# Two late edits in a fused RWKV attention and cosine feed-forward kernel: the last two half copies change buffers and order, and six checks with their vote move to an earlier place

## The chip, the cores and the metric

The kernel runs on one core of one Trainium2 chip. A core has five engines that each work through a queue in order: TensorE (PE, with its weight loads shown as PEld), VectorE (DVE), ScalarE (ACT), GpSimd (POOL) and SyncE (SP), whose queue here only issues DMA transfers. The metric is device microseconds (us) of one execution.

## The reference, cut to what matters

Batch 4, 8 heads, 768 steps, head size 48. A linear attention with decay `w` gives 3072 rows of 384 values; these go through a feed-forward layer of width 2048 whose gate is `h * cos(h)`:

```
state_t = w_t * state_(t-1) + k_t v_t ;  y_t = r_t (state_(t-1) + u k_t v_t)
h = x @ w_in ;  out = (h * cos(h)) @ w_out
```

The fast way of computing the decay is valid only for some inputs. So the kernel also looks at all of `w` (is any absolute value over 1?) and at the chunks' products of decays (is any too small?). A vote over both decides at the very end, in one branch that every engine takes, whether a slow loop over single steps redoes the whole output. With the inputs here it does not.

## The kernel before, in words

The 3072 rows are 24 chunks of 128 steps, two chunks to a block. A block's feed-forward is 8 units of 256 hidden columns, so there are 96 units. After a start written out token by token, the loop at L788 runs through **slots** t = 16 to 97. Slot t holds the first products of unit t (`mm1`, L577) and the second products of unit t - 2 (`mm2`, L595). Between them stands the gate of the unit, six steps on three engines: I (ScalarE, L540, reads the product bank), S (VectorE, L543), N (ScalarE, a sine, L556), M (VectorE, L557, the last reader of the product bank), H (ScalarE, L170, writes `gs`) and L (GpSimd, two halves, L173). There are two product banks, so `mm1` of slot t + 2 needs M of slot t to be over.

The attention of later chunks is spread over the same slots by the rows of PLAN. On VectorE it is a backward scan `e` (L282), a reciprocal and a forward scan `f` (L287, L288), the products `k` and `r` (L299, L301), `u` (L320), the sum `c` (L324), the decayed state `d` (L357) and twelve masked copies `P` (L395), which put the scores into the `asb` buffers. On PE it is the scores (L381), and for each block once the *own products* (L462, L468, from `asb`) and the *past products* (L490, L496), both ahead of `mm1` in the seventh of every eight slots; for the last block that is slot 86. When a block's last unit is over, ScalarE copies the two accumulators out (`ob`, L609) and SP sends them.

In each queue of PE, VectorE, ScalarE and GpSimd the instructions stand in the order of the program (L781). Only SP's order and the choice of a free buffer are the planner's.

The search for a large `w` is `check_decays` (L526 to L532): six pieces of 768 KB, each loaded by SP into a buffer of the five-fold ring `tt`, which also holds the chunks' inputs. VectorE takes the maximum of the piece (L531) and merges it into `wmax` (L532). A piece is checked after the events of its slot: with CHECK = 12, in slots 84 to 89. `take_vote` has two parts. The first (slot 91) is three small VectorE instructions that make `vote` and `low` (L769, L771, L773). The second (slot 92) is two one-column products on PE into a bank `pv` (L762, L763), and two VectorE instructions that make `bad` (L765, L766), which the branch at the end reads.

In the trace, `mm1` of slot 79 starts at 419.70 us, of slot 80 at 423.89, of 81 at 428.08, of 82 at 432.26, of 83 at 436.45, of 84 at 442.23, of 85 at 446.53 and of 86 at 453.73.

The last block's second accumulator is copied out in halves of 192 columns: VectorE copies the left one into `ob` and ScalarE the right one into `other` (L606, L607), both buffers of the ring `rr`; SP and ScalarE each send one half.

Of the kernel before, what the change touches and what calls it, by code (L numbers as in the profile page):

```python
# [10 lines left out]
F32 = mybir.dt.float32  # L11
# [7 lines left out]
AF = mybir.ActivationFunctionType  # L19
ALU = mybir.AluOpType  # L20
ET = mybir.EngineType

C = 128
# [17 lines left out]
W_SCALE = 2.0 ** 8  # L41
# [46 lines left out]
LAST = "mm1 I S N M", "mm1 I S N M mm2 h l", "mm2 h l"  # L88
CHECK = 12
PAIR = "0011010101010101"  # L90
NEEDS = dict(decay="load", lr="load", lv="load", diag="lr", d="decay", a="decay diag", t="decay",
             o="a lv", s="t d lv", p="o d")
# [3 lines left out]
def rwkv_cos_ffn(ctx: ExitStack, tc: tile.TileContext, tr, tn, tv, u, ut, wts, w, rkw, vst, us, xs, out):  # L96
    nc = tc.nc
    NG = tr.shape[0]
    TRW = tr.shape[2]
    DM = out.shape[1]  # L100
# [12 lines left out]
    def bank(kind, shape, name):  # L113

        tags = BANKS[stage[0]]
        turn[kind] += 1
        return ps.tile(shape, F32, tag=tags[kind][turn[kind] % len(tags[kind])], name=name)
# [3 lines left out]
    def buf(tag, shape, dtype, name=None, pool=sb):  # L121
        return pool.tile(shape, dtype, tag=tag, name=name or tag, bufs=BUFS.get(tag, 1))
# [37 lines left out]
    def engines(codes):  # L160
        E.update({k: {"v": nc.vector, "p": nc.gpsimd, "a": nc.scalar, "s": nc.sync}[e] for k, e in codes.items()})
# [61 lines left out]
    atts, outs, xts, units, accs = {}, {}, {}, {}, {}  # L223
# [302 lines left out]
    def check_decays(n):  # L526

        ww = buf("tt", [128, w.shape[1] // WCH], F32, "ww")
        nc.sync.dma_start(out=ww, in_=w[:, n * w.shape[1] // WCH:(n + 1) * w.shape[1] // WCH])
        top = buf("top", [128, 1], F32)  # L530
        nc.vector.tensor_reduce(out=top, in_=ww, axis=mybir.AxisListType.X, op=ALU.max, apply_absolute_value=True)  # L531
        nc.vector.tensor_tensor(out=wmax, in0=wmax, in1=top, op=ALU.max)  # L532
# [49 lines left out]
    def mm2(t):  # L582
        i, u = seq[t]
        if u == 0:
            if i < 2:
                stage[0] = 1 if i else 2
            tags = ("a2", "h2") if i == 1 else ("acc0", "acc1")
            accs[i] = [ps.tile([C, 512], F32, tag=x, name="acc") for x in tags]
        gs = units.pop(t)
        todo = [(a, b, fi, j) for a, b in PASSES for fi in range(FU) for j in range(BLK)]  # L590
        at_end = i == NBLK - 1 and u == NU - 1
        if at_end:
            todo.sort(key=lambda x: x[3])
        for a, b, fi, j in todo:
            nc.tensor.matmul(out=accs[i][j][:, :DM], lhsT=gs[:, a, fi, j * C:(j + 1) * C],  # L595
                             rhs=wgt[u * FU + fi][:, 1, b],
                             start=u == 0 and fi == 0 and a == 0 and b == 0, stop=u == NU - 1 and fi == FU - 1 and a == 1)
        if u == NU - 1:
            if i == 1:
                stage[0] = 3  # L600
            for j in range(BLK):
                ob = buf("rr", [C, DM], F32, "ob")
                with tc.high_priority(offset=HP):
                    if at_end and j:
                        other = buf("rr", [C, DM], F32, "other")
                        nc.vector.tensor_scalar(out=ob[:, :DM // 2], in0=accs[i][j][:, :DM // 2], scalar1=1.0 / W_SCALE ** 2, scalar2=None, op0=ALU.mult)  # L606
                        nc.scalar.activation(other[:, DM // 2:], accs[i][j][:, DM // 2:DM], AF.Copy, scale=1.0 / W_SCALE ** 2)  # L607
                    else:
                        nc.scalar.activation(ob, accs[i][j][:, :DM], AF.Copy, scale=1.0 / W_SCALE ** 2)  # L609
                chunk = order[i * BLK + j]  # L610
                if at_end and j:
                    nc.sync.dma_start(out=out[chunk * C:(chunk + 1) * C, :DM // 2], in_=ob[:, :DM // 2])
                    nc.scalar.dma_start(out=out[chunk * C:(chunk + 1) * C, DM // 2:], in_=other[:, DM // 2:])
                else:
                    E["qo"].dma_start(out=out[chunk * C:(chunk + 1) * C, :], in_=ob)

# [8 lines left out]
    slots = len(seq)  # L625
# [34 lines left out]
    def up(n):  # L660

        if n == 0 and up1[0] < slots:
            if up1[0] - up1[1] > LAG + 1:
                up(1)
            mm1(up1[0])
            up1[0] += 1
        elif n == 1 and up1[1] < up1[0]:
            mm2(up1[1])
            up1[1] += 1

    def events(i, row, t):
        for e in row.split():
            n, _, d = e.partition("+")
            if e == "mm1":
                up(0)
            elif e == "mm2":
                if up1[1] <= t - LAG:
                    up(1)
            elif e in "ISNMHLhl":
                at = (e.upper(), t - e.islower())  # L680
                if at in parts:
                    parts.pop(at)()
            elif n in "efrkmucPKXnd":
                at = i * (1 if n in "Xn" else BLK) + int(d)
                for m in dict(e=("decay",), m=("diag",), d=("d",)).get(n, ()):
                    att(at, m)
                for key in dict(f=(("f", at), ("W", at)), c=(("c", at), ("A", at)), d=(("d", at), ("pp", at)),
                                X=[(x, (at, side)) for x in ("xh", "xl") for side in range(2)]).get(n, ((n, at),)):
                    if key in parts:
                        parts.pop(key)()  # L690
            else:
                att(i * (1 if n in "osp" else BLK) + int(d), n)
# [66 lines left out]
    def take_vote(last):  # L759
        if last:  # L760
            pv = bank("a", [C, 512], "pv")
            nc.tensor.matmul(out=pv[:1, 0:1], lhsT=told["vote"], rhs=ones[:, 0:1], start=True, stop=True)  # L762
            nc.tensor.matmul(out=pv[:1, 1:2], lhsT=ones[:R, 0:1], rhs=told["low"], start=True, stop=True)  # L763
            votes = cst.tile([1, 1], F32, name="votes")
            nc.vector.tensor_reduce(out=votes, in_=pv[:1, 0:2], axis=mybir.AxisListType.X, op=ALU.add)  # L765
            nc.vector.tensor_copy(out=bad, in_=votes)  # L766
            return
        told["vote"] = vote = cst.tile([128, 1], F32, name="vote")
        nc.vector.tensor_single_scalar(out=vote, in_=wmax, scalar=1.0, op=ALU.is_gt)  # L769
        least = cst.tile([R, 1], F32, name="least")  # L770
        nc.vector.tensor_reduce(out=least, in_=wholes.rearrange("p g a -> p (g a)"), axis=mybir.AxisListType.X, op=ALU.min)  # L771
        told["low"] = low = cst.tile([R, 1], F32, name="low")
        nc.vector.tensor_single_scalar(out=low, in_=least, scalar=LEAST, op=ALU.is_le)  # L773
# [7 lines left out]
    with tc.manual_schedule(engines={ET.PE, ET.DVE, ET.Activation, ET.Pool}):  # L781
        with tc.manual_schedule(engines={ET.SP}):
            nc.scalar.copy(out=mask, in_=maskf)
            for token in START.split():
                at_first(token)
        engines(LATER)
        up2 = up1[0]
        for t in range(up2, slots + LAG):  # L788
            n = t - up2
            if t == slots - 2:  # L790
                E["g0"] = nc.vector
            row = FIRST[n] if n < len(FIRST) else PLAN[t % NU]
            events(t // NU, row if t < slots - 2 else LAST[t - slots + 2] if t <= slots else "mm2", t)
            if t >= slots - CHECK and n_checked[0] < WCH:
                check_decays(n_checked[0])
                n_checked[0] += 1
            if t == slots - CHECK - 1:
                nc.vector.tensor_reduce(out=halves, in_=ident[:R96, :R96].rearrange("p (h d) -> p h d", d=HD),
                                        axis=mybir.AxisListType.X, op=ALU.add)
            if t in (slots - 5, slots - 4):  # L800
                take_vote(t == slots - 4)
        while up1[1] < slots:
            up(1)
    assert not parts, list(parts)
# [172 lines left out]
```

## Time and profile before

| what | us |
|---|---|
| median of three runs | 507.45 (505.34 to 508.76) |
| the profiled execution | 505.55 |
| its span | 503.8 |
| PE busy | 496.7 (99%) |
| DVE busy | 389.5 (77%) |
| ACT busy | 256.5 (51%) |
| POOL busy | 204.7 (41%) |

The span is the time from the first to the last recorded instruction of the profiled execution; 1.75 us lie outside it. Busy shares are means over the whole span. Times of day in the text are us from the start of the span.

### The profile page before, as it was taken

The page shows a single profiled execution, that of the slowest core. Times are in us where ns is not written, and L with a number is a line of the kernel's source. Part 1 is how long each engine was busy: PE and PEld are TensorE (multiplying, and loading weights), DVE is VectorE, ACT ScalarE, POOL GpSimd, SP SyncE. Part 2 cuts the span into 40 slices and gives each one's busy share as a digit, 9 for nine tenths or more (in the row PEclk, how much of TensorE's full clock was granted, in tenths as well). Part 3 has the DMA queues.
Part 4 walks back from the last instruction along what each step waited for, and adds up shares of the span by engine and source line. Part 5 has one row for each costly group of instructions (what it writes and reads, how often), then busy time and mean ns, then how long its engine had stood idle before and what let it go on. Part 6 is the DMA issues. An engine that isn't in the chain of part 4 may idle for free.

```text
span 503.8 us, 13400 instructions
## 1 busy us (share of the span) xinstructions
PE 496.7 (99%) x5654; PEld 482.6 (96%) x5654; DVE 389.5 (77%) x685; ACT 256.5 (51%) x444; POOL 204.7 (41%) x274
## 2 busy tenths in 40 slices
PE   8999999999999999999999999999999999999997
PEld 8889999999999999999999999999999999999997
DVE  7998999687979868868868957967957966587633
ACT  2889788525344444445445335435534545544543
POOL 4434646435445344335333424524623633423330
PEclk9999999999999999999999999999999999999999
DMA  8989540242141051051051132214205203013001
GB/s 284 411 315 337 224 161 2 64 163 96 54 174 64 1 196 62 3 196 62 1 176 53 33 125 72 64 50 147 65 8 188 64 2 126 33 63 129 31 2 35
DMA packets 17327, 54.64 MB, mean 108 GB/s; under 512 B 2032, under 2 KB 8688, under 8 KB 17264
## 3 DMA queue, kind: packets, MB, share of 16 engines
q1 hardware_dynamic: 17120, 53.64, 30.1%
q8 instruction: 46, 0.75, 0.6%
q14 instruction: 17, 0.14, 0.1%
q10 hardware_dynamic: 144, 0.10, 0.1%
HBM read 49.02 MB, written 4.72 MB: 107 GB/s over the span
## 4 chain that ended last, share of the span: by engine, by line
PE 75%; DVE 12%; issue 4%; DMA 3%; ACT 3%; POOL 1%; SPq 1%; ACTq 0%; DVEq 0%; POOLq 0%
PE acc L595 33%; PE ph L577 32%; PE pa L381 2%; DVE rr L543 2%; DVE rr L557 2%; DMA tt<-tr 2%; PE py L462 2%; DMA raw<-wts 1%; PE py L468 1%; DVE tt L288 1%; PE py L496 1%; DVE ee L282 1%; PE pst L427 1%; DVE asb L395 1%; PE pt L404 1%
## 5 line engine op out<-in xcount | busy, mean ns | idle before, releaser
L173 POOL TENSOR_TENSOR gs<-rr,gs 128x256 fp32r<-128x256 f32 x188 | 154.2, 840 | 231.4 <-ACT gs L170 209.8
L577 PE MATMUL ph<-xT,w 128*128 128x256 f32 x1728 | 219.8, 281 | 0.2 <-DVE w L204 0.2
L595 PE MATMUL acc<-w,gs 128*128 128x384 f32 x1152 | 216.2, 337 | 0.2 <-DVE rr L557 0.2
L577 PEld LDWEIGHTS ph<-xT,w 128*128 128x128 f32 x1728 | 212.6, 188 | 3.4 <-issue 1.2
L595 PEld LDWEIGHTS acc<-w,gs 128*128 128x128 f32 x1152 | 196.2, 188 | 1.1 <-issue 0.6
L556 ACT ACTIVATE rr<-rr,quarter 128x512 f32<-128x512 f32 x96 | 69.4, 723 | 87.1 <-DVE rr L543 86.9
L543 DVE SCALAR_TENSOR_TENSOR rr<-rr,ph 128x512 f32<-128x512 int32 x96 | 65.5, 682 | 51.6 <-ACT rr L540 49.9
L170 ACT CAST gs<-rr 128x512 fp32r<-128x512 f32 x88 | 54.6, 620 | 66.3 <-DVE rr L557 40.2
L540 ACT ACTIVATE rr<-ph 128x512 int32<-128x512 f32 x96 | 57.3, 596 | 51.8 <-PE ph L577 51.4
L557 DVE TENSOR_TENSOR rr<-rr,ph 128x512 f32<-128x512 f32 x96 | 65.5, 682 | 22.0 <-ACT rr L556 19.7
L334 POOL TENSOR_SCALAR_AFFINE_SELECT asb<-cd 128x512 f32<-128x512 f32 x48 | 35.5, 766 | 52.4 <-DVE cd L324 35.1
L395 DVE COPY_PREDICATED asb<-turned_mask,pa 64x128 f32<-64x128 uint8 (+1 forms) x108 | 33.6, 347 | 1.8 <-POOL asb L334 0.3
L282 DVE TENSOR_TENSOR_SCAN ee<-tt,one_e 112x516 f32<-112x516 f32 (+1 forms) x25 | 32.7, 1313 | 2.2 <-POOL asb L334 1.2
L288 DVE TENSOR_TENSOR_SCAN tt<-tt,inj 112x516 f32<-112x516 f32 x24 | 30.3, 1262 | 0.8
L173 DVE TENSOR_TENSOR xT<-py,xT 128x384 fp32r<-128x384 f32 x22 | 11.4, 552 | 21.2 <-ACT xT L170 21.2
L194 ACT ACTIVATE top<-raw 128x768 f16<-128x768 bf16 x16 | 17.4, 1090 | 3.7 <-DMA raw<-wts 2.6
L170 ACT CAST xT<-py 128x384 fp32r<-128x384 f32 x24 | 10.4, 483 | 17.1 <-PE py L496 17.0
L462 PE MATMUL py<-asb,v 128*32 128x128 f32 x384 | 18.0, 276 | 0.3 <-DVE asb L392 0.2
L468 PE MATMUL py<-asb,v 128*32 128x128 f32 x384 | 17.3, 273 | 0.0
L202 DVE CUSTOM_DVE_ANT_0 h<-h,top 128x1536 uint16<-128x1536 uint16 x16 | 16.1, 1005 | 0.9 <-ACT top L194 0.9
L170 ACT COPY past<-dd 48x192 f32<-48x192 f32 x40 | 14.0, 349 | 2.7 <-DVE dd L357 2.4
L381 PEld LDWEIGHTS pa<-tt 48*64 48x64 f32 x576 | 12.9, 133 | 2.2 <-issue 2.2
(90 smaller groups left out, 370.7 us busy)
## 6 DMA issues: line engine op xcount, KB each, us to landing
tt<-tr SPq DMA_DIRECT2D x22, 770.5 KB, 7.0
raw<-wts SPq DMA_DIRECT2D x16, 767.8 KB, 7.1
rk<-tn SPq DMA_DIRECT2D x18, 384.0 KB, 3.5
v<-tv SPq DMA_DIRECT2D x24, 224.0 KB, 3.6
ww<-w SPq DMA_DIRECT2D x6, 768.0 KB, 5.2
out<-ob SPq DMA_DIRECT2D x23, 192.0 KB, 2.0
tt<-tr SPq DMA_DIRECT2D x4, 256.0 KB, 3.5
tt<-tr SPq DMA_DIRECT2D x1, 258.5 KB, 3.2
```

The costliest lines, as they stand in the source:

```text
L170: (nc.scalar.copy if E[name] is nc.scalar else E[name].tensor_copy)(out=out, in_=in_)
L173: E[name].tensor_tensor(out=out, in0=full, in1=high.bitcast(F32), op=ALU.subtract)
L282: nc.vector.tensor_tensor_scan(out=ee[:, pairs].rearrange("p a t -> p (a t)")[:, ::-1], data0=wp[:, cols][:, ::-1], data1=one_e[:, pairs]. ...
L288: nc.vector.tensor_tensor_scan(out=wp[:, 0:W129], data0=wp[:, 0:W129], data1=inj.rearrange("p a t -> p (a t)"), initial=0.0, op0=ALU.mult, ...
L334: nc.gpsimd.affine_select(out=asb, in_=col.unsqueeze(2).to_broadcast([C, NP, C]), pattern=[[0, 4], [1, C]], compare_op=ALU.is_equal, fill= ...
L395: nc.vector.copy_predicated(*(which(x) for x in (a["asb", h], turned_mask, pa[h])))
L540: nc.scalar.activation(made["rr"].bitcast(I32), ph, AF.Copy, scale=INV2PI / W_SCALE, bias=0.25)
L543: nc.vector.scalar_tensor_tensor(out=made["rr"], in0=made["rr"].bitcast(I32), scalar=-2.0 * math.pi * W_SCALE, in1=ph, op0=ALU.mult, op1=A ...
L556: N=lambda: nc.scalar.activation(made["rr"], made["rr"], AF.Sin, scale=1.0 / W_SCALE, bias=quarter),
L557: M=lambda: nc.vector.tensor_tensor(out=made["rr"], in0=made["rr"], in1=ph, op=ALU.mult), H=high, L=low)
L577: nc.tensor.matmul(out=ph[:, fi], lhsT=wgt[u * FU + fi][:, 0, a, kt * 128:(kt + 1) * 128], rhs=xT[:, b, kt], start=n == 0, stop=n == 3 * K ...
L595: nc.tensor.matmul(out=accs[i][j][:, :DM], lhsT=gs[:, a, fi, j * C:(j + 1) * C], rhs=wgt[u * FU + fi][:, 1, b], start=u == 0 and fi == 0 a ...
```

## The change

The two halves of the last accumulator go to two new buffers of 192 columns from the ring `asb` instead of two from `rr`. ScalarE's copy now stands ahead of VectorE's in the program. CHECK becomes 17, so the six pieces of `w` are checked after the events of slots 79 to 84. The two parts of the vote stand ahead of the events of slots 85 and 86, so the vote's two products are on PE's queue directly in front of the last own products. The small reduction that makes `halves` moves with CHECK from slot 83 to slot 78.

```
-CHECK = 12
+CHECK = 17
...
-                ob = buf("rr", [C, DM], F32, "ob")
+                if not (at_end and j):
+                    ob = buf("rr", [C, DM], F32, "ob")
                 with tc.high_priority(offset=HP):
                     if at_end and j:
-                        other = buf("rr", [C, DM], F32, "other")
-                        nc.vector.tensor_scalar(out=ob[:, :DM // 2], in0=accs[i][j][:, :DM // 2], scalar1=1.0 / W_SCALE ** 2, scalar2=None, op0=ALU.mult)
-                        nc.scalar.activation(other[:, DM // 2:], accs[i][j][:, DM // 2:DM], AF.Copy, scale=1.0 / W_SCALE ** 2)
+                        at_last = [buf("asb", [C, DM // 2], F32, "at_last") for n in range(2)]
+                        nc.scalar.activation(at_last[1], accs[i][j][:, DM // 2:DM], AF.Copy, scale=1.0 / W_SCALE ** 2)
+                        nc.vector.tensor_scalar(out=at_last[0], in0=accs[i][j][:, :DM // 2], scalar1=1.0 / W_SCALE ** 2, scalar2=None, op0=ALU.mult)
...
-                    nc.sync.dma_start(out=out[chunk * C:(chunk + 1) * C, :DM // 2], in_=ob[:, :DM // 2])
-                    nc.scalar.dma_start(out=out[chunk * C:(chunk + 1) * C, DM // 2:], in_=other[:, DM // 2:])
+                    nc.sync.dma_start(out=out[chunk * C:(chunk + 1) * C, :DM // 2], in_=at_last[0])
+                    nc.scalar.dma_start(out=out[chunk * C:(chunk + 1) * C, DM // 2:], in_=at_last[1])
...
             if t == slots - 2:
                 E["g0"] = nc.vector
+            if t in (slots - 11, slots - 10):
+                take_vote(t == slots - 10)
             row = FIRST[n] if n < len(FIRST) else PLAN[t % NU]
             events(t // NU, row if t < slots - 2 else LAST[t - slots + 2] if t <= slots else "mm2", t)
...
-            if t in (slots - 5, slots - 4):
-                take_vote(t == slots - 4)
```

## Rows read from the trace of the kernel before

**Rows 1.** The page: busy time of PE, granted clock in 40 slices.
```profile
PE 496.7 (99%) x5654; PEld 482.6 (96%) x5654; DVE 389.5 (77%) x685; ACT 256.5 (51%) x444; POOL 204.7 (41%) x274
...
PEclk9999999999999999999999999999999999999999
```

**Rows 2.** Chain of waits, from 440 us: start, length, engine, output, line, count.
```profile
450.88 0.57 PE py L462 x16
...
458.19 2.10 PE ph L577 x18
...
483.31 0.12 PE pv L762 x2
...
483.48 2.30 PE ph L577 x18
...
500.43 0.37 DVE ob L606
...
500.82 0.33 ACT other L607
```

**Rows 3.** Timeline of VectorE, slots 79 to 84: start, length, instruction, idle before.
```profile
424.11 0.69 DVE L557 TENSOR_TENSOR rr<-rr,ph 128x512 f32<-128x512 f32 x1 [0.32 <-ACT rr L556]
424.71 1.23 DVE L282 TENSOR_TENSOR_SCAN ee<-tt,one_e 112x516 f32<-112x516 f32 x1
...
428.30 0.69 DVE L557 TENSOR_TENSOR rr<-rr,ph 128x512 f32<-128x512 f32 x1
...
429.11 1.23 DVE L288 TENSOR_TENSOR_SCAN tt<-tt,inj 112x516 f32<-112x516 f32 x1
...
432.56 0.69 DVE L557 TENSOR_TENSOR rr<-rr,ph 128x512 f32<-128x512 f32 x1
...
433.75 0.55 DVE L324 TENSOR_REDUCE cd<-rk 128x8 f32<-128x384 f32 x1
...
441.53 0.35 DVE L357 TENSOR_TENSOR dd<-all_states,ee 112x192 f32<-112x192 f32 x1
441.80 0.24 DVE L798 TENSOR_REDUCE halves<-ident 96x2 f32<-96x96 f32 x1
441.96 3.94 DVE L395 COPY_PREDICATED asb<-turned_mask,pa 128x256 f32<-128x256 uint8 x12
445.94 0.69 DVE L543 SCALAR_TENSOR_TENSOR rr<-rr,ph 128x512 f32<-128x512 int32 x1
447.42 0.69 DVE L557 TENSOR_TENSOR rr<-rr,ph 128x512 f32<-128x512 f32 x1 [0.79 <-ACT rr L556]
```

**Rows 4.** Timeline of VectorE, one check in slot 86 and the S behind it.
```profile
458.85 1.74 DVE L531 TENSOR_REDUCE top<-ww 128x1 f32<-128x1536 f32 x1
...
461.13 0.68 DVE L543 SCALAR_TENSOR_TENSOR rr<-rr,ph 128x512 f32<-128x512 int32 x1
```

**Rows 5.** Timeline of VectorE, first and last instruction of the vote's first part.
```profile
479.86 0.14 DVE L769 TENSOR_SCALAR vote<-wmax 128x1 f32<-128x1 f32 x1
...
480.20 0.15 DVE L773 TENSOR_SCALAR low<-least 112x1 f32<-112x1 f32 x1
```

**Rows 6.** Busy time by engine in one stretch: length, PE, PEld, DVE, ACT, POOL, clock.
```profile
424.71:450.75 26.04, 26.04 (x239) 25.53 (x237) 18.50 (x37) 12.31 (x21) 10.37 (x15) 1.00 0.05 16
```

**Rows 7.** Timelines of ScalarE and PE: the accumulators' copies in slot 81, `mm2` in slot 82.
```profile
432.43 0.85 ACT L609 ACTIVATE ob<-acc 128x384 f32<-128x384 f32 x2
...
434.36 2.25 PE L595 MATMUL acc<-w,gs 128*128 128x384 f32 x12
```

**Rows 8.** SP's queue: two loads of `w`; and the page's median time to landing.
```profile
415.37 0.82 SPq L529 DMA_DIRECT2D ww<-w  x2
...
ww<-w SPq DMA_DIRECT2D x6, 768.0 KB, 5.2
```

**Rows 9.** Timeline of PEld at the start: the same filler product, first and second time.
```profile
1.87 6.63 PEld L723 LDWEIGHTS filled<-ident 128*128 128x128 f32 x38 [1.87 <-POOL ident masks.py:199]
...
9.31 1.20 PEld L723 LDWEIGHTS filled<-ident 128*128 128x128 f32 x10
```

## The prediction

> **What bounds the kernel now.** I read the page's busy times first. [...] VectorE is busy 77% of the span, but that is a mean; the change puts work on VectorE into one stretch, so that stretch is read next: its timeline over slots 79 to 84 [rows 3], what a check costs [rows 4], how much room there is [rows 6].
>
> **The tail.** Before, VectorE's half takes 0.37 us from 500.43 and ScalarE's 0.33 us from 500.82, one behind the other although their halves and buffers differ [rows 2]. [...] The swap keeps the sum of 0.70 us and changes which queue sends last. The gain lies between 0 and the 0.4 us of one copy; I take 0.1, since both halves still leave one copy apart. The new `asb` buffers cost nothing: their last readers are the own products of slot 86, over some 45 us earlier. Two `rr` buffers fall away unnoticed, since VectorE's copy already started 0.02 us after the last product.
>
> **The vote's products.** In slot 92 they take 0.17 us (483.31 to 483.48), and the `mm1` behind takes 2.30 us where others take 2.10 [rows 2]: 0.37 us. In front of the own products they still take 0.17; the slower `mm1` behind own and past products exists there already. That is a gain of 0.20 at most, if their operands are ready when PE arrives.
>
> **Are they?** PE comes to the last own products at 450.88 [rows 2]. The vote needs all six checks. VectorE's queue keeps the program's order, so they lie between the attention work of slots 79 to 84, which stays. One check costs 2.28 us there, from its start to the S behind it (458.85 to 461.13) [rows 4]. A late VectorE has three more distances to keep [rows 3]: from S to M 1.48 (445.94 to 447.42; the sine between them is ScalarE's, and k or r fits into the gap), from M to the next instruction 0.60 (424.11 to 424.71), and for a scan 1.23. Walking the queue:
>
> - Slot 79: M at 424.11, the scan ends at 425.94, a check brings S of slot 80 to 428.22.
> - Slot 80: M 429.70; the forward scan begins 0.81 behind M (428.30 to 429.11) and ends at 431.74; with the check, S of slot 81 comes at 434.02.
> - Slot 81: M 435.50; `c` begins 1.19 behind it and takes 0.55 [rows 3]; check; S of slot 82 at 439.52.
> - Slot 82: M 441.00, check from 441.60, S of slot 83 at 443.88.
> - Slot 83: M 445.36, the decayed state 0.27 (441.53 to 441.80), check from 446.23, masked copies from 448.51, where they began at 441.96.
> - Slot 84: the copies hold VectorE 3.98 (441.96 to 445.94); S 452.49, M 453.97, the last check from 454.57 to 456.85.
> - Slot 85: the vote's first part takes 0.49 (479.86 to 480.35) [rows 5]: ready at 457.34.
>
> So PE, due at 450.88, waits 6.5 us, and everything on its queue waits with it: own and past products, `mm1` of slot 86, `mm2` of slot 84. Nothing later gives this back, for PE has no idle time to lose. The checks that leave slots 85 to 89 free VectorE, which did not hold PE up there.
>
> A bound from below: between 424.71 and 450.75 VectorE idles 26.04 - 18.50 = 7.5 us [rows 6]. Five more checks are 11.4 us, the vote 0.5; less `halves` (0.2) and the S of slot 85 (0.5) that fall out of the stretch, 11.2 us. Were every idle moment filled, 3.7 us would stay over. It can't be filled: in slots 82 to 84 nothing lies between S and M, and each M waits 0.79 us for the sine (the row at 447.42 is one of three) [rows 3]. That makes 6.1, near the walk. I take 6.5 and keep 3.7 as the low end.
>
> **Smaller steps.** M late holds the product banks: M of slot 81 ends at 436.2, just as `mm1` of slot 83 starts (436.45). ScalarE's copies of the accumulators come 0.63 behind slot 81's sine, which now starts at 434.74; they end near 436.2, while `mm2` of slot 82 wants the accumulators at 434.36 [rows 7]. So PE may stand 1.9 us there already. This comes out of the 6.5 and is not added: the vote's time is VectorE's queue alone. H and L slip with M and still end ahead of their `mm2`, since PE slips as well. Behind the vote, VectorE's reduction of `pv` stands between M of slot 85 and S of slot 86, both later than the products; it costs PE nothing. The move of `halves` (0.24) to slot 78 is hidden by VectorE's idle time and relieves slot 83. On SP, pieces two and three are issued at 415.37 and a piece lands in 5.2 us [rows 8], ahead of their checks at 431.7 and 437.2. Pieces four to six take the buffers of pieces one to three, free after the checks near 427.7, 433.5 and 439.0, and land some 8 us ahead of need. The output transfers share SP's queue with them and can slip by a few us; the ring `rr` holds seven buffers for about three live units and two outputs, which covers that.
>
> **The sum.** +6.5 for the wait, +0.17 for the products there, -0.37 in slot 92, -0.1 at the tail: +6.2 us, from 505.55 to 511.75 in the profiled execution's own terms. That execution lies 1.9 us under the median of 507.45 and near the lowest of three. Against the mean of the four known times (505.34, 505.55, 507.45, 508.76), 506.8, the sum gives 513.0, and that is my number.
>
> **Rivals.**
>
> *The clock falls behind the wait.* PE would idle for 4.6 to 6.5 us in one piece; the trace's start shows such an idle time of 1.87 us. Behind it the same filler product took 6.63 / 38 = 174 ns, against 120 ns when it comes again [rows 9]: 38 x 54 ns = 2.1 us lost after idling, though the clock's row reads 1.00 there too. Repeated, it gives 513.0 + 2.1 = 515.1. [...]
>
> *The vote is in time.* If VectorE can take the checks out of order, or into its idle time, to be ready by 450.88, PE never waits. For it speaks that VectorE is idle 29% of that stretch. Against it: the 3.7 us that stay over even then, and a queue in program order. It decides at a vote before 450.88. The gain is 0.2 for the products and 0.1 to 0.4 at the tail: 506.8 - 0.4 = 506.4, not slower than before.
>
> *A piece of `w` comes late.* If the planner gives the fourth to sixth piece a buffer later than I think, or SP's queue holds them behind an output, VectorE waits in the middle of the attention work and the vote comes later still. With the 8 us of room above, a piece must slip by over that; each us beyond it is one more on the sum; with three of them, 516.
>
> **How the numbers follow.** The wait with the clock at 1.00: 45%, 513.0. The wait and a lower clock: 33%, 515.1. The vote in time: 17%, 506.4. A late piece: 5%. About 1% (5 us) can be told from no change. The first case is 1.2% up, so it passes that line some 7 times in 10; the second nearly always; the third never. Slower by over 1%: 0.32 + 0.31 + 0.04 = 0.67. Faster by over 1%: 0.02, for something that I don't see. Within: 0.31. The range starts at the small wait of 3.7 us on a fair base (506.8 + 3.4 = 510.2), less the 1.5 us by which runs lie under their mean: 508.7, and ends at 515.1 and the 2 us by which they lie over it: 517.
>
> **What would show it.** Right: in the changed profile PE idles for several us right ahead of the vote's products (`pv`), released by VectorE's `low`; the masked copies start near 448.5, not 442; a digit of PE's row near 90% of the span falls. The chain of waits goes through VectorE between 424 and 457. The last copies still follow each other, ScalarE first. Wrong: `pv` near 450.9 with no wait, or VectorE's masked copies at their old place; then the checks found room that I deny them. A clock digit under 9 behind the wait decides the first rival.

## The result: 1.4% slower, most of it a wait where the prediction placed it

The changed kernel takes 513.16 us (median of six runs, 512.65 to 514.33) against 505.72 for six runs of the kernel before: ratio 1.0139, 95% interval 1.0113 to 1.0165. The prediction was 513.0, slower. The profiled execution took 512.66 us with a span of 511.0, 7.2 us more than before.

The page after, to be held beside [rows 1]:

```profile
PE 499.3 (98%) x5654; PEld 485.2 (95%) x5654; DVE 389.3 (76%) x685; ACT 257.0 (50%) x444; POOL 204.6 (40%) x274
...
PE   8999999999999999999999999999999999979996
PEclk9989999999999999999999999999999999989999
```

A 7 stands in PE's row in the 36th slice, where 9 was, and the granted clock dips there too. (The clock's third digit dips too: 0.50 from 28 to 29 us. That is over 420 us ahead of the wait, so it has nothing to do with it.) The chain of waits over that place, to be held beside [rows 2]: start, length, engine, output, line, count.

```profile
452.99 1.76 DVE top L531
454.76 0.55 DVE wmax L532
455.33 0.15 DVE vote L770
455.49 0.17 DVE least L772
455.68 0.17 DVE low L774
...
455.89 0.19 PE pv L764 x2
456.08 0.57 PE py L462 x16
456.65 0.85 PE py L468 x16
457.51 0.43 PE py L462 x8
...
459.21 0.84 PE py L490 x16
460.05 0.60 PE py L496 x32
460.65 2.30 PE ph L577 x18
...
506.91 0.34 ACT at_last L607
507.28 0.36 DVE at_last L608
```

The chain now passes through VectorE: last check, vote, and only then PE. The sixteen products on L468 take 0.85 us where they took 0.44 before the change; the eight on L462 behind them 0.43 instead of 0.22. What PE waited for from 400 us on (engine, line, waited for: total, times, longest):

```profile
PE pv L763 <- DVE vote L770: 3.6, 1, 3.6
PE acc L595 <- ACT ob L610: 0.3, 1, 0.3
```

And the stretches around it (length, busy time and count of PE, PEld, DVE, ACT, POOL, then the granted clock):

```profile
450.00:451.85 1.85, 1.85 (x12) 1.75 (x11) 1.54 (x4) 0.23 (x1) 0.00 (x0) 1.00 0.00 0
451.85:455.60 3.75, 0.23 (x2) 0.00 (x0) 3.15 (x5) 1.62 (x3) 1.41 (x2) 1.00 0.00 0
...
456.08:460.65 4.57, 4.57 (x113) 4.00 (x112) 1.24 (x4) 1.34 (x2) 1.41 (x2) 0.63 0.01 4
460.65:462.95 2.30, 2.30 (x19) 2.30 (x20) 1.02 (x2) 0.87 (x2) 0.00 (x0) 1.00 0.00 0
```

Of the 3.75 us up to 455.60 PE works for 0.23, the end of its `mm2`, and stands still for 3.5, while VectorE works for 3.15. When PE starts again, its clock is granted at 0.63 on the mean of the next 4.57 us, at 0.50 from 456.65 to 459.21; from 460.05 on it is back at 1.00. Before, the same 113 records took 2.92 us (450.88 to 453.80).

Where the 7.2 us of span lie, each from the starts of the same instruction in both traces:

| stretch | us |
|---|---|
| ahead of slot 79 (M of slot 79 at 424.49, before 424.11), not by the change | +0.38 |
| slot 82: `mm2` waits for ScalarE's copies of the accumulators; the load for `mm1` of slot 83 starts at 437.47, before 436.28, less the 0.38 | +0.81 |
| from there to the start of the own products (456.08, before 450.88): wait for the vote and its products | +4.01 |
| own and past products, 4.57 instead of 2.92 | +1.65 |
| `mm1` of slot 86 to the last product's end, 46.24 instead of 46.61 | -0.37 |
| last product's end (506.89, before 500.41) to the span's end | +0.72 |

### The profile page after: what moved, and what is told of

Same layout as the page of the kernel before. It is cut to its first block, busy times and chain, and to the rows that moved or that the text cites. A ratio compares the mean times of both kernels' runs of the same rounds, so it can differ in the third digit from the quotient of the medians.

```text
span 511.0 us, 13397 instructions
## 1 busy us (share of the span) xinstructions
PE 499.3 (98%) x5654; PEld 485.2 (95%) x5654; DVE 389.3 (76%) x685; ACT 257.0 (50%) x444; POOL 204.6 (40%) x274
## 4 chain that ended last, share of the span: by engine, by line
PE 74%; DVE 16%; ACT 4%; issue 2%; POOL 1%; DMA 1%; SPq 1%; ACTq 0%; DVEq 0%
PE ph L577 32%; PE acc L595 31%; DVE rr L543 3%; DVE rr L557 2%; PE py L462 2%; PE pa L381 2%; PE py L468 2%; DVE tt L288 2%; DVE top L531 2%; DVE asb L395 2%; ACT rr L556 1%; DVE ee L282 1%; PE pst L427 1%; PE pt L404 1%; PE py L496 1%
## 5 line engine op out<-in xcount | busy, mean ns | idle before, releaser
L468 PE MATMUL py<-asb,v 128*32 128x128 f32 x384 | 18.2, 284 | 0.0
L462 PE MATMUL py<-asb,v 128*32 128x128 f32 x384 | 18.1, 282 | 0.0
```

## Experiments

All ratios are to the kernel before, run beside on the same chip.

**Is it the vote, or VectorE's lateness in itself?** The first run leaves the checks early and puts the vote back.

```
-            if t in (slots - 11, slots - 10):
-                take_vote(t == slots - 10)
...
+            if t in (slots - 5, slots - 4):
+                take_vote(t == slots - 4)
```

> The changed kernel, but the vote's two parts stand at their old places (slots 91 and 92); the six checks stay in slots 79 to 84. Theory (PE waits for the vote alone): VectorE is as late as in the changed kernel, its masked copies again near 447 to 451 us, yet PE comes to the own products near 452 without a wait over 0.3 us and the granted clock stays at 1.00. Left over against the kernel before: about 0.8 us in slot 82 and whatever the tail costs (0.7 us by the changed kernel's trace): some 507, ratio 1.002 to 1.004. Rival (VectorE's lateness holds PE by the masked copies or by M of slot 84, whatever the vote does): PE waits 3 us or more at the own products or at mm1 of slot 86, and the time stays over 510.

Measured: 507.84 us, ratio 1.0036 (1.0018 to 1.0053). VectorE is late as foretold, in its timeline:

```profile
448.71 3.92 DVE L395 COPY_PREDICATED asb<-turned_mask,pa 128x256 f32<-128x256 uint8 x12
```

and yet PE comes to its own products without a wait, 1.1 us behind the copies' end (chain of waits):

```profile
453.74 0.57 PE py L462 x16
454.32 0.44 PE py L468 x16
```

So the late masked copies are harmless; the products that need the vote are not. What is left, 1.8 us by the ratio, holds the wait of slot 82 (the trace has PE's wait for `ob` again) and the longer tail, 0.8 and 0.7 us.

**Is it VectorE's sum, or the place of the two small products?** All as in the change, but each check looks at half its piece.

```
-        nc.vector.tensor_reduce(out=top, in_=ww, axis=mybir.AxisListType.X, op=ALU.max, apply_absolute_value=True)
+        nc.vector.tensor_reduce(out=top, in_=ww[:, :w.shape[1] // WCH // 2], axis=mybir.AxisListType.X, op=ALU.max, apply_absolute_value=True)
```

> The changed kernel, but each check takes the maximum over only the left half of its piece of w, so half of w is not looked at; all else stays. A check should cost about 0.87 us less on VectorE, six of them 5.2 us. Theory (the sum of VectorE's queue sets the vote): low is ready 5 us earlier, near 450.8, and PE, due near 451 to 452, waits at most 0.3 us; the clock stays at 1.00; some 506, ratio 1.000 to 1.003. Rival (the place of the two small products in front of the own products costs by itself): the wait in front of pv goes but a delay of over 1 us stays there, 508 or more.

Measured: 506.82 us, ratio 1.0024 (1.0008 to 1.0040). PE's only wait after 380 us:

```profile
PE pv L763 <- DVE vote L770: 0.4, 1, 0.4
```

The wait shrinks from 3.6 to 0.4 us, a little over the 0.3 that was expected, and the own and past products behind it take 2.91 us (2.92 before the change). What is left, 1.2 us by the ratio, holds this wait and a longer tail (SP's half lands 2.6 us after its issue here; see below). So the wait comes from the six checks ahead of the products and not from the products' place.

**Does the clock fall because PE stands still?** Fourteen products that nobody reads fill the wait.

```
             pv = bank("a", [C, 512], "pv")
+            for again in range(FILL):
+                nc.tensor.matmul(out=pv[:, 128:256], lhsT=ident, rhs=ident, start=True, stop=True)
```

> The changed kernel with 14 products of the identity with itself (128x128, results not used) on PE right in front of the vote's products, some 3.4 us of work in the wait that is there. Theory (the clock falls because PE idles in the wait): the vote's products still run near 455.6 us, no earlier, but the granted clock stays at 1.00 and the own and past products take 2.9 us instead of 4.6: 1.6 us less than the changed kernel, some 511.5, ratio 1.011. Rival (the slow own and past products have another cause, VectorE or the small products ahead of them): they take 4.6 us again and the ratio stays 1.014.

Measured: 510.54 us, ratio 1.0087 (1.0065 to 1.0110). Its chain of waits:

```profile
455.73 0.19 PE pv L767 x2
455.92 0.56 PE py L463 x16
456.48 0.44 PE py L469 x16
```

The stretch of its own and past products (columns as above):

```profile
455.92:458.82 2.90, 2.90 (x113) 2.50 (x112) 1.23 (x4) 1.34 (x2) 0.27 (x1) 1.00 0.03 6
```

The vote comes at the same time as in the change, but the products behind it take 2.90 us at a granted clock of 1.00 instead of 4.57 at 0.63. More work on PE made the kernel faster, by 1.67 us in that stretch of the trace. The ratio fell by more, by 0.0052 or 2.6 us, but the two intervals nearly meet (1.0110 and 1.0113), so the size is taken from the trace.

**What is the early place worth by itself?** The kernel before with the vote early and nothing else; the vote sees one piece of six.

```
+            if t in (slots - 11, slots - 10):
+                take_vote(t == slots - 10)
...
-            if t in (slots - 5, slots - 4):
-                take_vote(t == slots - 4)
```

> The kernel before (CHECK = 12, old tail), but the vote's two parts stand ahead of the events of slots 85 and 86; so the vote sees only the first of the six pieces of w. Theory: low is ready near 450.8 us, when PE comes to the own products, so PE waits 0.2 us at most; the two small products add 0.17 us there and take 0.37 us from slot 92: between 0.2 us faster and no change, ratio 0.9985 to 1.0010. Rival (the early place holds PE in itself): PE waits 1 us or more in front of pv, ratio over 1.002.

Measured: 505.47 us, ratio 0.9985 (0.9971 to 1.0000). In its timelines `low` is ready at 453.38 and `pv` starts behind it with the 0.25 us that PE also takes at that place in the kernel before:

```profile
453.41 0.09 PEld L762 LDWEIGHTS pv<-ones,vote 128*1 128x1 f32 x2 [0.25 <-issue]
```

No wait, as the theory has it. The gain of 0.2 us lies inside the interval, whose upper end is 1.

**The tail.** The changed kernel's end has half of a surprise in it: SP's half lands 2.4 us after its issue (transfers from 500 us: count, KB, median us to landing).

```profile
out<-at_last ACTq DMA_DIRECT2D x1, 96.0 KB, 1.7
out<-at_last SPq DMA_DIRECT2D x1, 96.0 KB, 2.4
```

In the kernel before the two took 1.6 (SP) and 1.7 us. Five runs take the tail apart. The first has the kernel before with the whole tail edit; the second only swaps the two copies (`other` ahead of `ob`); the third only takes the `asb` buffers, VectorE's copy first.

> The kernel before with the changed tail alone: half copies in the asb buffers, ScalarE first. From the end of the last product to the end of the span it was 3.4 us before and 4.1 us in the changed kernel, where SP's half landed 2.4 us after its issue instead of 1.6. Theory (the tail edit itself costs 0.7 us): 4.1 us again, ratio 1.0005 to 1.0025. Rival (the prediction's 0.1 us gain holds, and the longer landing comes from elsewhere in the changed kernel or from chance): 3.2 to 3.4 us, ratio 0.999 to 1.000.

> The kernel before with ScalarE's half copy ahead of VectorE's, both still in rr buffers. If the order makes SP's transfer late (it is then the last one issued): landing 2.4 us, tail 4.1 us. If the asb buffers do it: landing 1.6 us, tail 3.3 us.

> The kernel before with the two halves in asb buffers of 192 columns, VectorE's copy still first. If the buffers make SP's transfer late: landing 2.4 us. If the order does it: SP's lands 1.6 us after issue, ScalarE's 1.7, tail 3.4 us as before.

Measured: ratios 1.0003 (0.9987 to 1.0018), 1.0002 (0.9984 to 1.0020), 1.0003 (0.9988 to 1.0018). SP's half lands after 1.6 us in all three; the first one's line:

```profile
out<-at_last SPq DMA_DIRECT2D x1, 96.0 KB, 1.6
```

So both answers that I offered for the order or the buffers fell: neither makes the transfer late, nor both together. Two more runs cross the tail with the rest of the change: the changed kernel with the old tail, and the kernel with the early vote and late checks with the new tail.

> The changed kernel with the tail of the kernel before (rr buffers, VectorE's half copy and SP's transfer first); checks and vote early as in the change. If the early checks make SP's last transfer late whatever the tail is: SP's half lands 2.4 us after its issue, and since it is issued 0.4 us ahead of ScalarE's, the tail is 3.7 us instead of 4.1 and 3.4. If only early checks together with the new tail do it: landing 1.6, tail 3.4 us, and 0.7 us less than the changed kernel. Either way PE waits 3.6 us for the vote and the ratio is 1.011 to 1.014.

> The kernel before with the vote early (slots 85 and 86, so that the vote sees one piece of six) and the changed tail; the checks stay in slots 84 to 89. If the early checks are what makes SP's last transfer land late: 1.6 us here, tail 3.4 us, ratio 0.998 to 1.001. If the early vote together with the new tail does it: 2.4 us, tail 4.1 us.

Measured: 511.74 us, ratio 1.0118 (1.0088 to 1.0149), and 505.41 us, ratio 0.9986 (0.9968 to 1.0005). SP's half lands after 1.6 us in both. The stall of the first is the changed kernel's (PE waits 3.6 us for the vote, the clock falls to 0.63 on the mean of the products behind it), its tail the old one: 3.4 us from 508.84 to 512.3. Over all traces, one of each kernel, the late landing (2.4 to 2.6 us) is there in all five kernels with early checks and the new tail, and in none of these five, which have only one of them or part of the tail edit. So it goes with the two together, 0.7 us in the trace.

The DMA records show what holds SP's half, which goes out as 128 packets of 768 bytes and 16 of 4 bytes. In the changed kernel, from 508.5 to 509.6 us, and in the early vote with the new tail, from 501.6 to 502.1 us, the stretches that hold these packets (queue, kind: packets, MB, share of the 16 DMA engines):

```profile
q1 hardware_dynamic: 144, 0.10, 27.6%
q8 instruction: 1, 0.02, 7.3%
q14 instruction: 2, 0.02, 7.0%
...
q1 hardware_dynamic: 144, 0.10, 60.9%
q10 hardware_dynamic: 17, 0.01, 5.0%
```

In the changed kernel an 8 KB transfer of the kind "instruction" on queue 14 starts at 508.67, while the half is on its way, and ends at 509.30. Of the half's packets 120 have started by 508.91; the other eight start from 509.30 on. It is the same in all five kernels with the late landing: the instruction transfer begins 0.1 to 0.3 us after the half's first packet, and the last eight packets begin at its end (505.67, 503.01, 507.59 and 504.45 in the other four). In the eight other traces, the kernel before among them, it begins 0.1 to 0.5 us after the half's last packet. Eight of 128 is the share of one of 16 engines, so the eight seem to stand behind the instructions on one engine; the record doesn't name the engine. No run moved the instruction transfer alone, and why it meets the half only when both edits are there stays open.

**How the wait's length counts, and what a merge costs.** Each check writes its maximum to a column of its own, and the vote reduces the six columns.

```
-        top = buf("top", [128, 1], F32)
-        nc.vector.tensor_reduce(out=top, in_=ww, axis=mybir.AxisListType.X, op=ALU.max, apply_absolute_value=True)
-        nc.vector.tensor_tensor(out=wmax, in0=wmax, in1=top, op=ALU.max)
+        nc.vector.tensor_reduce(out=wtops[:, n:n + 1], in_=ww, axis=mybir.AxisListType.X, op=ALU.max, apply_absolute_value=True)
```

> The changed kernel, but each check writes its maximum into a column of its own and the six columns are reduced once in the vote; the six merges into wmax (0.16 to 0.55 us each) are gone. Theory (VectorE's queue sets the vote, and a merge beside GpSimd's low part waits for that to end): low comes 1.2 to 1.6 us earlier, near 454.4, PE waits 2.0 to 2.6 us there instead of 3.6. If the granted clock falls after any wait of 2 us, own and past products take 4.6 us again and the ratio is near 1.011; if this shorter wait leaves it at 1.00, 2.9 us and 1.007. Rival (the long merges are only how the record shows a wait for something else): low comes at most 0.6 us earlier.

Measured: 509.01 us, ratio 1.0068 (1.0044 to 1.0091). PE's wait:

```profile
PE pv L761 <- DVE vote L769: 2.0, 1, 2.0
```

The stretch from the vote's products to the end of the past products, with the clock at 1.00 (the own and past products alone take 2.91 us, from 452.89):

```profile
452.60:455.80 3.20, 3.13 (x117) 2.70 (x115) 1.53 (x5) 1.34 (x2) 0.27 (x1) 1.00 0.02 5
```

Counted from slot 79's scan, `low` starts 28.64 us later instead of 30.58: 1.94 us earlier, more than the 1.2 to 1.6 expected: the three short merges cost as well, 0.2 us each (from check to next instruction 1.64 to 1.66 us in slots 79 to 81, instead of 1.84 to 1.86). A wait of 2.0 us leaves the clock at 1.00; that saves the 1.65 us once more. Wait and clock together make the ratio that was expected for this case, 1.007.

**Can it be had without the wait?** The same, with the old tail and the checks where VectorE has room.

```
-CHECK = 12
+CHECKS = 19, 18, 17, 16, 14, 13
...
-            if t >= slots - CHECK and n_checked[0] < WCH:
+            if slots - t in CHECKS:
```

> A whole version, nothing left out: the checks stand in slots 77, 78, 79, 80, 82 and 83, their merges are left to the vote, the vote is early as in the change, the tail is the old one. Theory (VectorE's queue ahead of the vote is all that is wrong with the change): compared with the run whose merges were left to the vote, where PE waited 2.0 us, one check less lies in slots 81 to 84 and two lie in slots with room; low is ready before PE comes to the own products, PE waits 0.3 us at most, the clock stays at 1.00. The gain over the kernel before is then the 0.2 us of the vote's products: ratio 0.998 to 1.001. Rival (VectorE waits for the second piece of w in slot 78, which lands near 422 us, and stays late): PE waits over 1 us, ratio over 1.002.

Measured: 505.85 us, ratio 1.0004 (0.9986 to 1.0023). `low` starts at 449.48, 0.9 us ahead of the vote's products, and the chain runs through PE alone:

```profile
450.42 0.12 PE pv L760 x2
450.54 0.03 PE pv L761
450.56 0.49 PE py L462 x14
```

This is the whole computation with an early vote, and it neither loses nor gains anything that can be measured: from the start of the vote's products to the last product's end it takes 49.2 us, where the kernel before takes 49.5 from the own products on.

## Why the prediction was right, and where not

*The mechanism.* Right. VectorE's queue sets the vote and PE waits for it with everything behind, 3.6 us in the trace; a late M or late copies don't hold PE, beyond the 0.8 us of slot 82. The first, second and last runs show it from three sides.

*The wait's size.* 6.5 us foretold, 4.65 measured (0.81 in slot 82 and 4.01 ahead of the own products, less the vote's 0.17, which is a term of its own). The term that was wrong is the price of a check: 2.28 us, taken from [rows 4]. From VectorE's timeline in the changed kernel:

```profile
426.24 1.73 DVE L531 TENSOR_REDUCE top<-ww 128x1 f32<-128x1536 f32 x1
428.00 0.16 DVE L532 TENSOR_TENSOR wmax<-wmax,top 128x1 f32<-128x1 f32 x1
428.08 0.69 DVE L543 SCALAR_TENSOR_TENSOR rr<-rr,ph 128x512 f32<-128x512 int32 x1
...
442.24 0.55 DVE L532 TENSOR_TENSOR wmax<-wmax,top 128x1 f32<-128x1 f32 x1
...
447.05 3.82 DVE L395 COPY_PREDICATED asb<-turned_mask,pa 128x256 f32<-128x256 uint8 x12
```

From each check to the next instruction it took 1.84, 1.85, 1.86, 2.25, 2.00 and 2.34 us, 12.1 in sum instead of 13.7. That is 1.5 of the 1.9 us by which the walk was too long (33.2 us from M of slot 79 to the end of `low`, measured 31.3); the rest is 0.1 us each in the two scans' distances, the copies and `c`. A check in another neighbourhood was another check: its short merge took 0.57 us in [rows 4], up to the end of GpSimd's pair, and 0.16 in slots 79 to 81, with no such pair beside it (last section).

*The bound.* The 3.7 us below held: 4.65 lies between it and the walk.

*Slot 82.* Foretold as 1.9 us out of the wait, measured 0.81, for the same reason: VectorE was less late.

*A late piece of `w`.* No check waited for its piece: VectorE has no idle time ahead of any L531 in these slots.

*The clock.* The prediction's likeliest case (45%) left it at 1.00, and this was the step that failed; the rival, given 33% and 515.1 us, came true, though PE stood for 3.6 us in one piece and not for 4.6 to 6.5. Its price of 2.1 us from [rows 9] measured 1.65. That it came near is partly luck: the granted clock is 1.00 in those rows, so they show no fall of the clock, and a wait of 2.0 us, as long as the idle time ahead of them, left the clock at 1.00 in the run with the merges in the vote. The fill-in run shows that here standing still is the cause: with the wait filled, the products behind it took 2.90 us at 1.00 instead of 4.57 at 0.63. The first sixteen of them took 0.57 us even behind the wait, as in the kernel before (last section).

*The vote's products.* -0.37 us in slot 92 as foretold, and no cost of the place.

*The tail.* A gain of 0.1 us foretold, a loss of 0.72 measured. Alone, the edit is worth nothing that can be measured (1.0003). The swap kept the sum of 0.70 us, since the copies still go in turn, 0.34 us from 506.91 and 0.36 from 507.28; why they do no run shows. That SP's transfer would land later, 2.4 us after its issue instead of 1.6, while a transfer of instructions ran, was not foreseen.

*The number.* The sum was +6.2 on a base of 506.8. Measured were +7.4 on 505.72. That 513.0 lies so near to 513.16 is partly luck: wait too long by 1.9, clock and tail short by 2.5, 0.4 ahead of slot 79 in no term, base high by 1.1.

## What to carry to other kernels

Here instructions that could run any time before the end became a deadline when a busy queue carried them ahead of needed work, and PE waited 3.6 us: walk the producer's queue to that place with the moved work in it, not the engine's mean busy share. Take the price of a moved instruction from several neighbourhoods (the same merge took 0.16 us in one and 0.55 in another, beside GpSimd). Count the slower clock behind a long stall of the busiest engine as part of the stall (here 1.65 us behind 3.6, nothing behind 2.0). And when the last transfer lands late (here after 2.4 us instead of 1.6), look at what else the DMA engines carry just then before blaming its buffer or its place.

## What the runs showed of the hardware that was not expected

The 128x1 merge of two buffers on VectorE ends with GpSimd's low part of the gate where the two meet. In the kernel before, six merges took 0.54 to 0.57 us, and each ends when GpSimd's pair of subtractions ends. From GpSimd's timeline, a pair that ends at 461.19:

```profile
459.75 1.44 POOL L173 TENSOR_TENSOR gs<-rr,gs 128x256 fp32r<-128x256 f32 x2 [5.08 <-ACT gs L170]
```

From VectorE's, the merge that ends at 461.20:

```profile
460.63 0.57 DVE L532 TENSOR_TENSOR wmax<-wmax,top 128x1 f32<-128x1 f32 x1
```

In the changed kernel the merges at 428.00, 433.29 and 438.29 have no such subtraction beside them and take 0.16 us; those at 442.24, 446.84 and 454.76 end with it and take 0.55, 0.29 and 0.53. It is so in all eleven traces that have the merges: the 54 beside a subtraction end within 0.03 us of its end and take 0.29 to 0.68 us, the 12 without one take 0.16.

The clock did not fall during the wait (1.00 from 451.85 to 455.60) but behind it: in the changed kernel the first sixteen own products still took 0.57 us, as before the change, and the next sixteen 0.85 instead of 0.44; so it goes on until 460.05. With the old tail the weights of the first 32 products were still loaded in 0.41 and 0.48 us, as in the early vote with the new tail, where PE has no wait. A wait of 2.0 us left the clock at 1.00; two waits of 3.6 us, in the changed kernel and in the one with the old tail (0.63 over its 4.6 us of own and past products), did not.
